# Assumed landing times of DMAs by kind of transfer in a scheduled forward-and-backward kernel

## The chip, the cores and the metric

The kernel runs on one core of a Trainium2 chip. Its time is the device time in microseconds of one execution; smaller is better. Before the change four executions took 803.83, 809.00, 809.76 and 813.18 us, median 809.38 us. One execution was profiled.

## The reference

A forward pass and the gradients of all its inputs. In the forward pass x has shape (2, 16000, 256), in bfloat16. Two convolutions over time of width 3, each followed by the tanh form of GELU and by keeping every second step, bring it to 4000 steps; then comes a joint of every step with eight vectors g:

```
h  = gelu(conv3(x, w1))[:, ::2]          # 2 x 8000 x 256
f  = gelu(conv3(h, w2))[:, ::2]          # 2 x 4000 x 256
fe = f @ w_f ;  ge = g @ w_g
j  = tanh(fe[:, :, None] + ge[:, None])  # 2 x 4000 x 8 x 256
out = j @ w_o
```

The outputs are out and, from grad_out of out's shape, the gradients of x, w1, w2, g, w_f, w_g and w_o. A gradient of a weight is a product over time: it wants time on the partitions of both operands. A product along the layer wants channels there. So most tensors are needed in both layouts, and the kernel turns them with DMA transposes.

## The kernel before, in words

**Tiling.** The 2 x 4000 steps are cut in 18 chunks. Chunk 0 has 256 steps, chunks 1 to 7 have 512, chunk 8 has the 160 that end batch 0; chunks 9 to 15 have 512, chunk 16 has 256 and chunk 17 has 160. Three stages work on different chunks at once. `stage_a` computes the convolutions and fe of the next chunk (XC is x in column layout, HT the first layer, FT the second, FE is fe). `stage_j` treats the joint of the current chunk in four pairs of the eight vectors: JT is j by columns, made on ScalarE (ACT), JR is j by rows, made by a sum on VectorE (DVE) and a tanh on ACT; GO_R is a piece of grad_out as loaded and GOT the same transposed. Products with WOT (from GOT) go into a sum over the eight vectors, ZS, and the last sum is NGFE, the negative gradient of fe. GWO collects the gradient of w_o in PSUM over the whole program. `stage_de` takes the chunk before through the layers backwards (GF, GH) and adds up the weight gradients ACCF, ACC2 and ACC1.

**Transposes.** All are issued from SyncE's (SP's) queue. FER is fe by rows, for JR. NFR, GFR and GHR are the gradients NGFE, GF and GH by rows; FR and HR are FT and HT by rows, kept from the forward pass until the gradients meet them. XC comes transposed from x in HBM, GOT from GO_R in SBUF. Plain loads (GO_R, X9 and X5, which are x by rows) and stores (OUT_SB, GX_SB, w_out) go through the same queue.

**Order.** Nothing is ordered by hand. Each operation is recorded with its engines, an assumed cost and its buffers; `Flow.issue` runs a model of the engines forwards (`run`) and backwards (`backward`) a few times and emits the program in the order of the best pass. In that model a compute operation may follow when its inputs are ready and a wake-up time has passed; an operation that would have to wait is treated as if it could start `SLACK` ns later than it could, so others are taken first. A DMA counts as landed when the queue's own share of its work is done, 2000 ns have passed and a margin has passed too:

```
o.done = ring[e] + 2000.0 + o.margin
```

The margin is `MARGIN` unless the call gives another (the first loads have `FIRST` or 2000 ns). It delays the readers in the planned order, and the moment at which a stored buffer is taken for free. It puts no wait in the program: on the chip everything waits on semaphores, in the order planned. An operation with two possible engines (copies out of PSUM, the squares JSQ) goes where the model has room.

Each class of buffers has a few slots: three for GOT, four for GO_R and w_out together, one for GHR. A transfer into a slot waits for the last reader of what was in it.

**The end.** In the last chunk `acc_add` writes each weight gradient as w_out on DVE and stores it; there are seven such stores. `store` writes two more.

Of the kernel before, what the change touches and what calls it, by code (L numbers as in the profile page):

```python
# [13 lines left out]
ACT = mybir.ActivationFunctionType  # L14
# [8 lines left out]
FIRST = 500.0  # L23
# [20 lines left out]
class Flow:  # L44
# [1 line left out]


    WAKE = {"PE": 45.0, "ACT": 25.0, "DVE": 25.0, "POOL": 280.0, "SP": 60.0}
    SLACK = {"PE": 800, "ACT": 300, "DVE": 300, "POOL": 0.0, "SP": 0.0}
    MARGIN = 4500.0  # L50
    TAIL = {"PE": 180.0, "ACT": 130.0, "DVE": 95.0, "POOL": 40.0, "SP": 0.0}

    def __init__(self, ctx, tc):
# [221 lines left out]
def c_dve(n, f=1.0):  # L275
    return 66.0 + 1.042 * n * f
# [3 lines left out]
def kernel(  # L280
# [27 lines left out]
    KT = 2  # L308
    P = 128
# [25 lines left out]
    F = Flow(ctx, tc)  # L335
# [99 lines left out]
    def dma(q, out, in_, r, w, bytes_, new=(), transpose=False, at=None, after=(), cost=None, hold=(), nb=None, margin=None):  # L435
        def go(e):
            eng_ = nc.sync if e == "SP" else nc.gpsimd if e == "POOL" else nc.scalar
            if transpose:
                return eng_.dma_start_transpose(out=out(), in_=in_())
            else:  # L440
                return eng_.dma_start(out=out(), in_=in_())
        c = 1260.0 if transpose else 400.0 if q == "SP" else cost or (750.0 if q == "POOL" else 100.0)
        return op(q, c, go, r=r, w=w, new=new, at=at, after=after, hold=hold, nb=nb, margin=margin,
                  work=bytes_ / 256 * 1.25 if transpose else bytes_ / 300.0)
# [6 lines left out]
    def load_xc(g_, at):  # L451
        b, ci, c0, W = chunks[g_]
        nb, wh, S = nb_of[g_], whole[g_], st[g_]
        XC = buf("jt", [P, 4 * KT * 2 * P], BF16, "XC0") if g_ == 0 else buf("xc", [P, 4 * KT * CW], BF16, "XC")
        if wh:
            vw = lambda: XC.t[:, 0:nb * 4 * KT * P].rearrange("p (a c k q) -> p a c k q", a=nb, c=4, k=KT)
            S["xcol"] = lambda c, kt: vw()[:, :, c, kt, :]
            S["xback"] = [(P, lambda kt: vw()[:, 0:nb - 1, 3, kt, :])]
            last_cols = lambda lo, hi: vw()[:, nb - 1, 3, :, lo - (nb - 1) * P:hi - (nb - 1) * P]
            src = x[b, 4 * c0:4 * (c0 + W), :].rearrange("(p r) d -> p (r d)", r=4 * nb)  # L460
            n = 2 * 4 * KT
            S["XCd"] = [dma("SP", lambda h=h: XC.t[:, h * n * P:(h + 1) * n * P].rearrange("p (g q) -> p g q", q=P),
                            lambda h=h: src[:, h * n * P:(h + 1) * n * P], r=[], w=[(XC, ("m", h))],
                            bytes_=n * P * P * 2, new=[XC] if h == 0 else [], transpose=True, at=at,
                            margin=FIRST if g_ < 2 else None) for h in range(nb // 2)]
            S["XCk"] = [(XC, ("m", h)) for h in range(nb // 2)]
        else:
            vw = lambda: XC.t[:].rearrange("p (g w) -> p g w", g=4 * KT)
            S["xcol"] = lambda c, kt: vw()[:, c * KT + kt, 0:W]
            S["xback"] = [(P, lambda kt: vw()[:, 3 * KT + kt, P - 1:W - 1])]  # L470
            last_cols = lambda lo, hi: vw()[:, 3 * KT:4 * KT, lo:hi]
            S["XCd"] = [dma("SP", lambda: vw()[:, :, 0:W], lambda: xr[b, c0:c0 + W, :], r=[], w=[(XC, ("m", 0))],
                            bytes_=W * 4 * D * 2, new=[XC], transpose=True, at=at)]
            S["XCk"] = [(XC, ("m", 0))]
        if ci > 0:
            xh = st[g_ - 1]["XH"]
            XS = shift("xs", g_, "XS", last_cols, [S["XCk"][-1]], lambda: xh[:], [xh], at=at)
        else:
            XS = shift("xs", g_, "XS", last_cols, [S["XCk"][-1]], None, [], at=at)
        S["xback"] = [(0, lambda kt: XS[:, kt, :])] + S["xback"]  # L480
        if c0 + W < MQ:
            XH = S["XH"] = buf("xh", [P, KT, 1], BF16, "x_halo")
            op("POOL", 200.0, lambda e: nc.gpsimd.tensor_copy(out=XH[:], in_=last_cols(W - 1, W)),
               r=[S["XCk"][-1]], w=[XH], new=[XH], at=at)
        S["XC"], S["XS"] = XC, XS
# [141 lines left out]
    def dma_rows(name, cls, g_, src, reads, n, nb=None, at=None):  # L627

        R = buf(cls, [P, KT * n * P if cls == "hrs" else KT * NB * P], BF16, name)
        R.view = lambda t_: t_[:, 0:KT * n * P].rearrange("p (k b q) -> p k b q", k=KT, q=P)  # L630
        R.rows = lambda m, bl: R[:m, :, bl, :]
        R.cols = lambda m, bl, d2: R[:m, d2, bl, :]
        dma("SP", lambda: R.t[:, 0:KT * n * P].rearrange("p (g q) -> p g q", q=P), src, r=reads, w=[R],
            bytes_=KT * n * P * P * 2, new=[R], transpose=True, nb=nb, at=at)
        return R

    def col_rows(name, cls, g_, SRC, keys, nb=None):
# [31 lines left out]
    def stage_a(g_, t0, dt):  # L669
# [4 lines left out]
        ns, nc_ = KT * (Wp + P), KT * Wp  # L674
# [13 lines left out]
        for nm, T_, k_, keys in (("HTo", HTo, (HT, "os"), [(HT, ("o", 0)), (HT, ("o", 1))]),  # L688
                                 ("G1o", G1o, (G1o, "s"), [(G1o, 0), (G1o, 1)])):
            if wh:  # L690
                op(("POOL", "DVE"), (430.0, c_dve(KT * (P - 1), 0.25)), lambda e, T_=T_: (
                    nc.gpsimd if e == "POOL" else nc.vector).tensor_copy(out=T_[:, :, 1:P], in_=T_[:, :, Wp:Wp + P - 1]),
                   r=keys, w=[k_])
# [4 lines left out]
            else:  # L698
                pv, pw, pk = st[g_ - 1][nm], P + chunks[g_ - 1][3], st[g_ - 1][nm + "k"]
                op("POOL", 200.0, lambda e, T_=T_, pv=pv, pw=pw: nc.gpsimd.tensor_copy(  # L700
                    out=T_[:, :, r0:r0 + 1], in_=pv[:, :, pw - 1:pw]), r=pk, w=[(k_[0], k_[1] + "h")])
# [21 lines left out]
        FE = colbuf("fe", g_, "FE")  # L723
        S["FE"] = FE
        n = nb_of[g_]
# [12 lines left out]
        if wh:  # L738
            FR_ = S["FER"] = buf("fer", [P, NB, D], BF16, "FER")
            dma("SP", lambda: FR_[:, 0:n].rearrange("p b (k q) -> p (b k) q", q=P), lambda: FE.t[:, 0:KT * n * P],  # L740
                r=[(FE, 0), (FE, 1)], w=[FR_], bytes_=KT * n * P * P * 2, new=[FR_], transpose=True)
        else:
            pad_tail(g_, FE)
            S["FER"] = to_rows("fer", FE, 0, n * P, [0, 1, "z"])
# [4 lines left out]
            bytes_=(ns + nc_) * P * 2, new=[HR], transpose=True, nb=late[0])  # L749
# [6 lines left out]
        else:  # L756
            R1 = buf("hrs", [P, KT * 2 * P], BF16, "HRs")
            assert nb_of[g_] == 2
            for kt in range(KT):
                dma("SP", lambda kt=kt: R1[:, kt * 2 * P:(kt + 1) * 2 * P].rearrange("p (g q) -> p g q", q=P),  # L760
                    lambda kt=kt: HTo[:, kt, P - 1:3 * P - 1],
                    r=[HT], w=[(R1, kt)], bytes_=2 * P * P * 2, new=[R1] if kt == 0 else [], transpose=True, nb=late[0])
            S["HRs"] = [R1], lambda m, bl, d2: R1[:m, d2 * 2 * P + bl * P:d2 * 2 * P + (bl + 1) * P]
        FR = col_rows("FR", "fr", g_, FT, ["z"], late[1])
# [147 lines left out]
    def acc_add(ACC, key, acc_ap, ps, g_, out):  # L912
        if g_ == NG - 1:
            t_ = buf("go", [P, NB, 2, V], BF16, "w_out")
            op("DVE", c_dve(512), lambda e: nc.vector.scalar_tensor_tensor(
                out=t_[:, 0].rearrange("p k d -> p (k d)"), in0=acc_ap().rearrange("p k d -> p (k d)"), scalar=-1.0, in1=ps[:],
                op0=ALU.mult, op1=ALU.subtract),
               r=[(ACC, key), ps], w=[t_], new=[t_])
            dma("SP", lambda: out.rearrange("(dt p) n -> p dt n", p=P),
                lambda: t_[:, 0], r=[t_], w=[], bytes_=131072)  # L920
        elif g_ == 0:
            evac(lambda: acc_ap().rearrange("p k d -> p (k d)"), lambda: ps[:], 512, r=[ps], w=[(ACC, key)])
        else:
            op("DVE", c_dve(512), lambda e: nc.vector.tensor_tensor(  # L924
                out=acc_ap().rearrange("p k d -> p (k d)"), in0=acc_ap().rearrange("p k d -> p (k d)"), in1=ps[:],
                op=ALU.add), r=[(ACC, key), ps], w=[(ACC, key)])

    def stage_de(g_, t0, dt):
# [9 lines left out]
        nc_ = KT * nb_of[g_] * P  # L938
# [9 lines left out]
        for mt in range(KT):  # L948
            ps = psum()

            def mms(e, mt=mt, ps=ps):
# [4 lines left out]
                out=GF[:, mt, 0:W], in0=S["G2"][:, mt, :W], scalar=1.0, in1=ps[:, :W], op0=ALU.add, op1=ALU.mult),  # L956
               r=[(S["G2"], mt), ps], w=[(GF, mt)])
# [5 lines left out]
        if not last:  # L963
            FH = S["GFh"] = buf("gfh", [P, KT, 1], BF16, "GF_halo")
            op("POOL", 200.0, lambda e: nc.gpsimd.tensor_copy(out=FH[:], in_=GF[:, :, W - 1:W]),
               r=[(GF, 0), (GF, 1)], w=[FH], new=[FH])
# [4 lines left out]
        for mt in range(KT):  # L971
            ps = psum()

            def mms(e, mt=mt, ps=ps):
# [9 lines left out]
                out=GHo[:, mt, 0:Ws], in0=S["G1o"][:, mt, r0:r0 + Ws], scalar=1.0, in1=ps[:, 0:Ws], op0=ALU.add, op1=ALU.mult),  # L984
               r=S["G1b"](mt) + [ps], w=[(GH, ("o", mt))])
# [3 lines left out]
            def mms2(e, mt=mt, ps=ps):  # L989
# [4 lines left out]
                out=GHe[:, mt, 0:W], in0=S["G1e"][:, mt, 0:W], scalar=1.0, in1=ps[:, :W], op0=ALU.add, op1=ALU.mult),  # L994
               r=[(S["G1e"], mt), ps], w=[(GH, ("e", mt))])
# [7 lines left out]
        if not last:  # L1003
            hh = S["GHh"] = buf("ghh", [P, KT, 1], BF16, "GHe_halo")
            op("POOL", 200.0, lambda e: nc.gpsimd.tensor_copy(out=hh[:], in_=GHe[:, :, W - 1:W]),
               r=[(GH, ("e", 0)), (GH, ("e", 1))], w=[hh], new=[hh])
# [28 lines left out]
        else:  # L1035
# [2 lines left out]
        ghk = [(GH, (k_, mt)) for k_ in "oe" for mt in range(KT)] + [(GH, "ez"), (GH, "oz")]  # L1038
        GHR = buf("ghr", [P, 2 * KT * CW], BF16, "GHR")
        dma("SP", lambda: GHR.t[:, 0:2 * nc_].rearrange("p (g q) -> p g q", q=P), lambda: GH.t[:, 0:2 * nc_], r=ghk, w=[GHR],  # L1040
            bytes_=2 * nc_ * P * 2, new=[GHR], transpose=True)
        for o_, nm in ((0, "GHoR"), (nc_, "GHeR")):
            R_ = S[nm] = part(GHR, lambda t_, o_=o_: t_[:, o_:o_ + nc_].rearrange("p (k b q) -> p k b q", k=KT, q=P))
            R_.rows = lambda m, bl, R_=R_: R_[:m, :, bl, :]
# [10 lines left out]
        for bl, m in sblk:  # L1055
# [28 lines left out]
            elif wh:  # L1084
                if head == 1:
                    dma(STOREQ, lambda: out_1[b, 1:5, :].rearrange("(o f) d -> o f d", o=1), lambda GX=GX: GX[0:1],
                        r=[gk(0), gk(1)], w=[], bytes_=2048, cost=550.0)
                for lo, hi in row_parts(head, P):
# [3 lines left out]
                        bytes_=(hi - lo) * 4096, cost=550.0)  # L1092
            else:
                for lo, hi in row_parts(r0, r1):
# [3 lines left out]
                        bytes_=(hi - lo) * 2048, cost=550.0)  # L1098
# [15 lines left out]
    def gg_out():  # L1114
# [43 lines left out]
       r=[(warm, 0)], w=[(warm, 1)])  # L1158
# [117 lines left out]
```

## Time and profile before

The profiled execution took 806.12 us; its span is 804.3 us.

| Engine | busy us | share of the span |
|---|---|---|
| TensorE, matmul (PE) | 772.1 | 96% |
| TensorE, weight loads (PEld) | 568.0 | 71% |
| VectorE (DVE) | 746.4 | 93% |
| ScalarE (ACT) | 696.7 | 87% |
| GpSimd (POOL) | 84.5 | 11% |

A chain of waits and works, followed back from the last instruction, puts 32% of the span on TensorE and 7% on DVE in what it shows. The queue of DMAs moved 187.81 MB. From issue to landing the median was 6.2 us for GOT, 5.2 for NFR, 5.9 for XC, 3.8 for FER, 4.1 for GFR and FR, 4.6 for GHR and 4.8 for HR.

In the lines of the profile a number with L is a line of the kernel (L413 is the matmul helper, L439 and L441 issue a transpose and a plain DMA). "ps<-NFR,FR" names what is written and read. "x8" counts instructions. In lists of waits the columns are the total, the number and the longest wait in microseconds. In a timeline the first column is the start and the second the duration; "[2.19 <-DMA NFR<-NGFE]" is idle time ahead of an instruction and what ended it. SPq is SP's queue of DMA issues; its bars are the issuing, and the landing comes later.

### The profile page before, as it was taken

To read this page: it belongs to the slowest core of one execution; us is meant where nothing else is said; L and a number is where in the kernel's file an instruction comes from. 1 tells how busy PE (TensorE), PEld (TensorE's weight loads), DVE (VectorE), ACT (ScalarE), POOL (GpSimd) and SP (SyncE) were. 2 spreads that over 40 slices of the span, in tenths; PEclk is the share of its full clock that TensorE was granted. 3 is DMA by queue.
4 is the path that set the end of the run, shared out by engine and by line. 5 is a ranking of instruction groups with operands and counts; after the bars stand their busy time and mean duration, and the time that the engine had idled before them with its cause. 6 is when DMAs were issued, how large, how long until landed. Compare 5 with 4: busy or idle time off the path is not lost. (4 is left out here: it accounts for less than half of the span.)

```text
span 804.3 us, 16636 instructions
## 1 busy us (share of the span) xinstructions
PE 772.1 (96%) x6004; PEld 568.0 (71%) x6004; DVE 746.4 (93%) x1702; ACT 696.7 (87%) x1150; POOL 84.5 (11%) x269
## 2 busy tenths in 40 slices
PE   7798999999898999999999989999999999999996
PEld 5455767686675867777776658676776867778885
DVE  3999999999988999998979999998999999999975
ACT  4999999998887998988778999988889989998762
POOL 2101010100101001011101110000001001001111
PEclk9999999999999999999999999999999999999999
DMA  8999999999999999999999999999999999999986
GB/s 193 201 257 207 240 200 238 245 214 265 231 222 231 240 268 220 268 225 227 254 230 199 238 231 235 256 236 239 261 237 253 236 285 233 252 245 241 215 208 164
DMA packets 419231, 187.81 MB, mean 234 GB/s; under 512 B 342182, under 2 KB 410828, under 8 KB 419148
## 3 DMA queue, kind: packets, MB, share of 16 engines
q1 hardware_dynamic: 416636, 185.54, 104.4%
q10 hardware_dynamic: 2384, 1.18, 0.6%
q8 instruction: 47, 0.77, 0.4%
q14 instruction: 36, 0.29, 0.1%
q0 software_dynamic: 128, 0.03, 0.0%
HBM read 51.56 MB, written 50.34 MB: 127 GB/s over the span
## 5 line engine op out<-in xcount | busy, mean ns | idle before, releaser
L800 ACT ACTIVATE JT<-FE,GE 128x512 bf16<-128x512 bf16 (+2 forms) x288 | 186.0, 699 | 1.0 <-DVE FE L429 0.9
L820 ACT ACTIVATE JR<-JR 128x1024 bf16<-128x1024 bf16 x128 | 137.3, 1081 | 20.3 <-DVE JR L813 20.1
L867 DVE SCALAR_TENSOR_TENSOR NGZ<-JSQ,ps 128x512 f32<-128x512 bf16 (+2 forms) x252 | 151.3, 606 | 2.8 <-PE ps L413 2.7
L413 PE MATMUL ps<-WO,JT 128*128 128x256 bf16 x1024 | 150.3, 273 | 3.2 <-ACT JT L800 2.1
L413 PE MATMUL ps<-GOT,WT 128*128 128x512 bf16 (+3 forms) x640 | 151.4, 333 | 1.8 <-DVE OUT_SB L429 1.2
L424 ACT CAST OUT_SB<-ps 128x512 bf16<-128x512 f32 x210 | 126.5, 615 | 24.0 <-PE ps L413 23.7
L413 PE MATMUL GWO<-GO_R,JR 128*128 128x256 bf16 x1024 | 135.4, 277 | 5.9 <-ACT JR L820 5.9
L875 DVE TENSOR_TENSOR ZS<-ZS,NGZ 128x512 f32<-128x512 f32 (+2 forms) x216 | 130.7, 611 | 0.7
L413 PEld LDWEIGHTS <-JT 128*128 128x128 bf16 x1024 | 98.4, 98 | 46.0 <-ACT JT L800 4.2
L413 PEld LDWEIGHTS <-JR 128*128 128x128 bf16 x1028 | 101.2, 99 | 31.2 <-ACT JR L820 7.7
L413 PEld LDWEIGHTS <-WT 128*128 128x128 bf16 x1000 | 88.4, 98 | 43.4 <-issue 5.6
L857 ACT ACTIVATE JSQ<-JT 128x1024 bf16<-128x1024 bf16 (+2 forms) x113 | 109.6, 972 | 7.0 <-DVE NGZ L867 6.4
L413 PEld LDWEIGHTS <-W 128*128 128x128 bf16 x720 | 66.8, 99 | 54.8 <-issue 4.4
L413 PE MATMUL ps<-WT,GH 128*128 128x256 bf16 x732 | 98.9, 273 | 0.1
L413 PE MATMUL ps<-XC,W 128*128 128x512 bf16 (+4 forms) x432 | 93.6, 346 | 2.6 <-DMA XC<-in_x_dram 2.6
L813 DVE TENSOR_TENSOR JR<-FER,GEB 128x1024 bf16<-128x1024 bf16 x128 | 87.1, 686 | 9.6 <-DMA FER<-FE 8.6
L413 PE MATMUL ps<-GHR,X 128*128 128x256 bf16 x768 | 91.5, 273 | 2.1 <-DVE NGZ L867 1.3
L413 PEld LDWEIGHTS <-X 128*128 128x128 bf16 x768 | 74.8, 98 | 13.1 <-issue 2.2
L605 DVE SCALAR_TENSOR_TENSOR g_s<-g_sq,ps 128x512 bf16<-128x512 bf16 (+2 forms) x108 | 65.7, 610 | 18.8 <-ACT HT L603 14.7
L413 PEld LDWEIGHTS <-GH 128*128 128x128 bf16 x732 | 71.2, 98 | 14.9 <-DVE GH L983 0.6
L601 ACT ACTIVATE g_sq<-ps 128x512 bf16<-128x512 f32 (+2 forms) x108 | 60.3, 558 | 19.9 <-PE ps L413 13.4
L924 DVE TENSOR_TENSOR ACC<-ACC,ps 128x512 f32<-128x512 f32 x96 | 64.2, 678 | 9.7 <-PE ps L413 9.2
(124 smaller groups left out, 964.4 us busy)
## 6 DMA issues: line engine op xcount, KB each, us to landing
GO_R<-in_grad_out_dram SPq DMA_DIRECT2D x56, 512.0 KB, 4.6
out_dram<-OUT_SB SPq DMA_DIRECT2D x56, 512.0 KB, 5.2
out_dram<-GX_SB SPq DMA_DIRECT2D x28, 512.0 KB, 3.5
X<-in_x_dram SPq DMA_DIRECT2D x14, 576.0 KB, 6.2
X<-in_x_dram SPq DMA_DIRECT2D x14, 512.0 KB, 6.8
GO_R<-in_grad_out_dram SPq DMA_DIRECT2D x8, 256.0 KB, 4.0
out_dram<-OUT_SB SPq DMA_DIRECT2D x8, 256.0 KB, 3.9
GOT<-GO_R SPq DMA_TRANSPOSE x72, 6.2
```

What stands on the lines that cost most here:

```text
L413: nc.tensor.matmul(ps_ap, lhsT=lhsT, rhs=rhs, start=start, stop=stop)
L424: nc.scalar.copy(out=dst(), in_=src())
L601: op("ACT", c_act(W, True), lambda e, mt=mt, ps=ps: nc.scalar.activation(out=sq[:, mt, :W], in_=ps[:, :W], func=ACT.Square, scale=GELU_SQR ...
L605: op("DVE", c_dve(W), lambda e, mt=mt, ps=ps: nc.vector.scalar_tensor_tensor(out=s[:, mt, :W], in0=sq[:, mt, :W], scalar=1.0, in1=ps[:, :W ...
L800: op("ACT", c_act(W, ptr=True), lambda e, j=j, mt=mt: nc.scalar.activation(out=S["blocks"](JT[:, j, mt, :W]), in_=S["fe"](mt), func=ACT.Ta ...
L813: op("DVE", c_dve(n * 2 * D, 0.5), lambda e, lo=lo, n=n, m=m, JR=JR: nc.vector.tensor_tensor(out=JR[:m, lo % 2:lo % 2 + n], in0=S["FER"][: ...
L820: op("ACT", c_act(n * 2 * D), lambda e, lo=lo, n=n, m=m, JR=JR: nc.scalar.activation(out=JR[:m, lo % 2:lo % 2 + n], in_=JR[:m, lo % 2:lo % ...
L857: nc.scalar.activation(out=JSQ[:, :, :W], in_=JT[:, j, :, :W], func=ACT.Square)
L867: op("DVE", c_dve(W) + 6, lambda e, d2=d2, ps=ps, u=u, zap=zap, JSQ=JSQ: nc.vector.scalar_tensor_tensor(out=zap(), in0=JSQ[:, d2, :W], sca ...
L875: op("DVE", c_dve(W), lambda e, d2=d2, dst=dst, NGZ=NGZ: nc.vector.tensor_tensor(out=dst[:, d2, :W], in0=ZS[:, d2, :W], in1=NGZ[:, :W], op ...
L924: op("DVE", c_dve(512), lambda e: nc.vector.tensor_tensor(out=acc_ap().rearrange("p k d -> p (k d)"), in0=acc_ap().rearrange("p k d -> p ( ...
```

## The change

Three constants and five calls are touched.

- `MARGIN` goes from 4500 to 3500 ns and TensorE's `SLACK` from 800 to 500 ns.
- A margin `LATE` of 8000 ns is new. It is given to XC from the third chunk on (in whole chunks), FER, NFR, GFR and GHR, and to what else `dma_rows` transposes, other than FR.
- The shorter `MARGIN` remains for GOT after the first chunk, GO_R, the row loads of x, FR, HR and all stores.
- The seven stores of `acc_add` are issued from ACT's queue instead of SP's, with an assumed cost of 450 ns.

```diff
-    SLACK = {"PE": 800, "ACT": 300, "DVE": 300, "POOL": 0.0, "SP": 0.0}
-    MARGIN = 4500.0
+    SLACK = {"PE": 500, "ACT": 300, "DVE": 300, "POOL": 0.0, "SP": 0.0}
+    MARGIN = 3500.0
+    LATE = 8000.0
...
-                            margin=FIRST if g_ < 2 else None) for h in range(nb // 2)]
+                            margin=FIRST if g_ < 2 else F.LATE) for h in range(nb // 2)]
...
-            bytes_=KT * n * P * P * 2, new=[R], transpose=True, nb=nb, at=at)
+            bytes_=KT * n * P * P * 2, new=[R], transpose=True, nb=nb, at=at, margin=None if name == "FR" else F.LATE)
...
-                r=[(FE, 0), (FE, 1)], w=[FR_], bytes_=KT * n * P * P * 2, new=[FR_], transpose=True)
+                r=[(FE, 0), (FE, 1)], w=[FR_], bytes_=KT * n * P * P * 2, new=[FR_], transpose=True, margin=F.LATE)
...
-            dma("SP", lambda: out.rearrange("(dt p) n -> p dt n", p=P),
-                lambda: t_[:, 0], r=[t_], w=[], bytes_=131072)
+            dma("ACT", lambda: out.rearrange("(dt p) n -> p dt n", p=P),
+                lambda: t_[:, 0], r=[t_], w=[], bytes_=131072, cost=450.0)
...
-            bytes_=2 * nc_ * P * 2, new=[GHR], transpose=True)
+            bytes_=2 * nc_ * P * 2, new=[GHR], transpose=True, margin=F.LATE)
```

Because the planner is run anew with these numbers, the order changes throughout the program on every engine, and some copies and squares go to another engine. The instructions' number and sizes stay the same, apart from where they run.

## The prediction

> **What bounds the kernel now.** I read the page's engine shares first, then the busy times stage by stage, then TensorE's waits, and last the timeline around the longest of them.
>
> ```profile
> PE 772.1 (96%) x6004; PEld 568.0 (71%) x6004; DVE 746.4 (93%) x1702; ACT 696.7 (87%) x1150; POOL 84.5 (11%) x269
> ...
> core 0: us, PE busy (x) PEld busy (x) DVE busy (x) ACT busy (x) POOL busy (x), PEclk, DMA share, GB/s
> 20.00:88.00 68.00, 57.48 (x390) 38.28 (x388) 64.83 (x162) 65.14 (x110) 7.52 (x20) 0.95 1.04 217
> 88.00:203.00 115.00, 115.00 (x849) 81.67 (x848) 112.51 (x236) 109.23 (x173) 11.02 (x30) 1.00 1.09 239
> 203.00:265.00 62.00, 57.31 (x413) 40.31 (x411) 56.02 (x117) 49.49 (x78) 6.94 (x20) 0.97 1.12 226
> 265.00:370.00 105.00, 105.00 (x849) 80.57 (x848) 103.57 (x230) 95.74 (x159) 10.06 (x34) 1.00 1.11 242
> 370.00:480.00 110.00, 104.97 (x823) 74.28 (x822) 99.35 (x239) 95.01 (x156) 13.16 (x42) 1.00 1.03 230
> 480.00:780.00 300.00, 299.38 (x2395) 227.24 (x2393) 287.57 (x659) 265.55 (x447) 28.13 (x96) 1.00 1.07 243
> ```
>
> TensorE never stops from 88 to 203, 265 to 370 and 480 to 780 us. Eight GWO matmuls of 256 columns follow each other in 0.87 us there (the chain), 0.109 us each; at that rate the whole program is 755 us of matmul. What can be won is idle time: 10.5 us from 20 to 88 (DVE and ACT full: a ramp), 4.7 from 203 to 265, 5.0 from 370 to 480, 0.6 after, 7.0 in the last 24.3. The middle ones have a name:
>
> ```profile
> PE ps L413 <- DMA NFR<-NGFE: 7.1, 3, 2.5
> PE GWO L413 <- ACT JR L820: 0.9, 2, 0.5
> PE ps L413 <- DVE g_sq L613: 0.7, 1, 0.7
> ...
> 187.71 0.69 DVE L875 TENSOR_TENSOR NGFE<-ZS,NGZ 128x512 bf16<-128x512 f32 x1
> ...
> 192.72 5.45 SPq L439 DMA_TRANSPOSE GOT<-GO_R  x1
> ...
> 198.27 0.56 SPq L441 DMA_DIRECT2D GO_R<-in_grad_out_dram  x1
> ...
> 198.89 0.62 SPq L441 DMA_DIRECT2D out_dram<-OUT_SB  x1
> ...
> 199.60 2.38 SPq L439 DMA_TRANSPOSE NFR<-NGFE  x1
> ...
> 206.96 1.05 PE L413 MATMUL ps<-NFR,FR 128*128 128x256 bf16 x8 [2.19 <-DMA NFR<-NGFE]
> ```
>
> NGFE is whole at 188.4 us; its transpose gets its turn on SP at 199.60, 11.2 us later, because SP issues DMAs back to back and is that far behind; it lands 7.3 us after. The plan allowed 2.0 + 4.5 us and the transfer's own work. It was 2.2 us short.
>
> **What the Trainium skill says.** "Perfetto Trace Analysis", DMA Instruction — HWDGE: the record of a DMA issue starts when its semaphores are satisfied and covers descriptor generation, not data movement. The trace agrees: the GOT issue at 185.44 lasts 6.10 us though its buffer was free at 175.9, so SP's bars are work and not waits. "TensorE: Matmul & The Clock Gate", What's actually happening: an idle window of about 3.4 us puts the array at half clock. Here the stall that ended at 256.4 us is followed by 256.5 to 260.3 us at a granted 0.55; those at 207 and 476 us, as long, by none. "DMA: Bandwidth & Descriptors", Issuing engines are not separate DMA queues: a second ring saves the sequencer's time only. No run of before shows it for these stores.
>
> **The change part by part.** The sum is made against the profiled execution: 806.1 us, span 804.3; the median of the runs is 809.4, 3.3 higher.
>
> *Late-needed transposes, 4.5 to 8.0 us (NFR, GFR, GHR, FER, XC).* The planner places the consumer 3.5 us later. In the order that the two builds give TensorE I added up the matmuls (0.109 us per 256 columns) between the last WOT product of a chunk, which NGFE needs, and the first matmul that reads NFR. It goes from 19.5 to 24.1 us in chunks 3 and 4, 16.2 to 19.5 in 7, 16.8 to 19.2 in 8, 16.1 to 20.0 in 9. These are the chunks that stalled; their stalls were 2.3, 2.7, 0.9, 0.3 and 2.6 us from start to start, so each is covered with 1.3 to 2.4 us to spare. The group of NFR matmuls shows 8.0 us of idle time in all, GHR in the middle 0.4; the half clock after 256.5 costs 3.8 x 0.45 = 1.7. Gone: 10.1 us. XC's margin costs nothing: by the landings its first reader comes 10 us or more after it past the ramp.
> What is late next: with TensorE 8 us faster SP has less time to catch up, and these stalls were its catching up. If SP's lag grows by the first stall removed (2.2 us), chunk 4 is at its limit. Bounds 0 to 5 us; I take 1.5, because from 480 to 780 us SP kept up with a TensorE that stood still for 0.6 us.
> FER: after the batch change DVE waited 2.5 us for it and ACT then 4.5 for JR; the work from FE to the first GWO product on JR goes from 15.6 to 21.1 us there, so the 0.9 us of GWO waits go: -0.9.
>
> *Loads ahead, 4.5 to 3.5 us (GOT, GO_R, X9, HR, FR, and the slots that stores free).* The dangerous one is GOT. Its longest way from a free buffer to landing is 9.5 us on SP and 9.0 more (free 175.9, issued 185.44, landed 194.4): 18.5. Matching landings with matmuls, GOT had 0.8 us left at its tightest in the steady part (issued 637.8), 2.5 and 2.7 at 593 and 624. The matmul work between the release and the first reader shrinks from 21.8 to 19.4 us at two of these places, which would leave -1.6 and 0.1. Against it, there the new order issues GOT ahead of HR, whose issue is some 3 us (3.05 at 633.39). Bounds 0 to 6 us (three short waits and a half clock); I take 1.5. GO_R lands 16.8 us or more before its matmul through the middle, HR and FR 23 or more: a shorter margin costs nothing while that stays.
>
> *TensorE's slack, 800 to 500 ns.* Products may follow their ACT or DVE producers 0.3 us closer. Such waits are now 0.9 + 0.7 + 0.6 us from 88 to 780. Bounds: 0 to 4 us; a gain isn't likely, as TensorE is full there anyway. I take 1.4.
>
> *Work between engines.* The planner moves 8 squares JSQ from DVE (31 to 23, 0.60 us each) to ACT (113 to 121, 0.95 each). DVE's queue is 6 us shorter, ACT's 7.6 longer. ACT is hidden (265.6 of 300 us busy at 480 to 780); its cost appears only where ACT is full, up to 140 us. Up to the end of chunk 1's gradient (NGFE at 97.3 us) DVE has 1.5 us less queued, ACT the same, TensorE 0.7 less: the ramp takes -1.0 (bounds -3 to +2; its PE stalls of 3.4 and 1.0 us may move).
>
> *The last gradients on ACT's ring.* Seven stores leave SP:
>
> ```profile
> 796.41 5.40 SPq L441 DMA_DIRECT2D out_dram<-w_out  x7
> ...
> DVE w_out L915 <- DMA out_dram<-w_out: 2.0, 2, 1.1
> ```
>
> SP had the GX_SB stores (794.97, 1.35 us) ahead of them. On ACT they stand behind four GX_SB copies, and nothing stands behind them. The first goes out up to 1.1 us sooner (its DVE result was there at 795.3), so the buffers that DVE waits for come free sooner; but the last product ends near 799.8 us and the last DVE step began at 800.7, so at most 0.7 can go. An ACT issue costs about what SP's does (0.38 to 0.66 us in the first 12 us, 0.4 on SP). The order before it changes as well: after the last WOT product TensorE has 12.6 us of matmul left instead of 11.3, but the X-gradients of the chunk before now stand between GH and GX, ahead of the last GHR transpose that needs their buffer. Followed step by step, these two cancel to 0.3 us. Together -0.6 (bounds -2 to +1.5).
>
> Sum: -10.1 + 1.5 - 0.9 + 1.5 + 1.4 - 1.0 - 0.6 = -8.2 us: 797.9 us for an execution like the profiled one. The runs of before spread over 9 us; if late landings make the spread, the added room draws the median towards the lower end, so I take the 3.3 us for gained too: **798 us**.
>
> **Rivals.** (1) *Forecast*, 798, 792 to 803: chance 0.55. (2) *SP is the real bound.* It is as full as TensorE, its lag is 6 to 11 us from 100 to 720, and no DMA work is removed; each stall taken from NFR comes back at the next transpose. A third of the gain stays: 809.4 - 3.4 = 806. For it: the lag of 11 us before every NFR stall. Against: 300 us at full rate with that lag steady. Chance 0.22. (3) *GOT becomes the stall, slower.* Every whole chunk has a GOT with about 19.4 us of cover; it decides when release to landing is over that, and 18.5 is already seen. At 1.6 us in each of 14 whole chunks that is +22 us, less the 10.1 won: 809 + 12 = 821. Against: only a few of the 72 had under 3 us. Chance 0.13. (4) *Nothing to see.* Both orders are full, the list is only shuffled and gains and new small waits cancel: 809. Chance 0.10.
>
> **How the numbers follow.** About 1% (8 us) is what a measurement of this kernel tells from no change. Faster by over 1% is under 801.3: most of case 1, 0.45, and the fast edges of the others, 0.05. Slower by over 1%: case 3 and a tail of 4, 0.15. The rest, 0.35, is within. The range reaches from case 1's lower end with no new wait at all (791) over case 2 and most of 4 (811); case 3 is left out.
>
> **What would show it.** NFR waits of TensorE under 2 us in sum; no half clock past 100 us; 203 to 265 us with under 1 us idle; SP's lag before NFR as before or longer; GOT waits of TensorE under 2 us; JSQ on DVE 23. I am wrong if TensorE waits for GOT in most chunks, if its waits for ACT and DVE grow past 4 us, or if the ramp up to 88 us loses over 3 us more.

## The result, and the profile after

The changed kernel takes 801.55 us (median of 44 executions, 797.37 to 807.66) against 808.44 us for the kernel before beside it (63 executions, 800.46 to 815.71). The ratio is 0.9934, 95% interval 0.9919 to 0.995: 0.7% less, 5.3 us by the ratio and 6.9 by the medians, where 8 to 11 were forecast. Here and below a median is over all executions of a kernel, while a ratio compares only those in the faster of the two states that executions of this kernel show, so it isn't the quotient of two medians. The profiled execution took 803.75 us, its span is 801.9 (before: 806.12 and 804.3).

Engine shares of the page, then busy times stage by stage, TensorE's waits from 88 to 780 us, and the timeline around the longest stall, all of the changed kernel:

```profile
PE 771.5 (96%) x6004; PEld 567.3 (71%) x6004; DVE 743.6 (93%) x1691; ACT 703.8 (88%) x1158; POOL 91.4 (11%) x272
```

```profile
20.00:88.00 68.00, 58.50 (x404) 39.23 (x402) 65.83 (x165) 66.16 (x111) 7.33 (x18) 0.95 1.04 220
88.00:203.00 115.00, 114.39 (x838) 80.64 (x837) 113.31 (x236) 109.21 (x171) 12.26 (x32) 1.00 1.08 237
203.00:265.00 62.00, 62.00 (x468) 45.18 (x467) 61.08 (x128) 54.92 (x86) 7.10 (x20) 1.00 1.08 241
265.00:370.00 105.00, 103.59 (x830) 78.58 (x828) 100.34 (x222) 91.97 (x155) 10.68 (x33) 1.00 1.09 238
370.00:480.00 110.00, 105.84 (x824) 75.00 (x823) 99.19 (x236) 98.47 (x163) 15.05 (x46) 0.98 1.03 233
480.00:780.00 300.00, 295.40 (x2364) 223.52 (x2362) 282.58 (x649) 266.79 (x443) 31.00 (x95) 1.00 1.09 242
```

```profile
PE ps L414 <- DMA GOT<-GO_R: 7.9, 4, 3.4
PE GWO L414 <- ACT JR L821: 1.4, 6, 0.3
PE ps L414 <- DVE NGZ L868: 0.6, 1, 0.6
PE ps L414 <- DVE OUT_SB L430: 0.4, 1, 0.4
PE ps L414 <- DVE NGFE L876: 0.2, 1, 0.2
```

```profile
391.44 5.98 SPq L440 DMA_TRANSPOSE XC<-in_x_dram  x2
397.52 0.53 SPq L442 DMA_DIRECT2D out_dram<-OUT_SB  x1
398.14 2.78 SPq L440 DMA_TRANSPOSE GHR<-GH  x1
401.01 1.93 SPq L440 DMA_TRANSPOSE GOT<-GO_R  x1
...
402.62 0.32 PE L414 MATMUL ps<-GOT,WT 128*128 128x128 bf16 x4
406.35 1.03 PE L414 MATMUL ps<-GOT,WT 128*128 128x512 bf16 x2 [3.41 <-DMA GOT<-GO_R]
```

The stall of 203 to 265 us is gone (62.00 of 62 us busy), and no wait for NFR is left in the list, where 7.1 us stood. In its place TensorE waits for GOT, four times, 7.9 us in all: 3.4 us up to 406.35 (after XC and GHR on SP, and 5.3 us to landing), 3.3 up to 598.6, and two short ones up to 359 and 646.5 (0.4 and 0.8). Behind the longest the granted clock is 0.61 from 406 to 410 us, which costs 1.6 us more; behind the one at 598.6 it is 1.00. So the waits for DMAs from 88 to 780 us are 7.9 us after as against 7.5 before (8.2 with one of 0.7 that the list puts down to DVE's g_sq, though what came last for that matmul was NFR).

In this pair of profiles TensorE's idle time from 88 to 780 us didn't fall at all: it is 10.3 us before and 10.8 after. The 2.4 us by which the span is shorter come from the ramp up to 88 us, where idle time fell by 1.0, from the end after 780 (1.2 less) and from busy time (0.6 less). In a second pair, e8 and e5 below, whose spans differ by 3.6, idle time from 88 to 780 fell from 17.7 to 14.0 us; both of these traces lack 44 of the matmul records, which makes their idle time too large. The removed stalls are certain; that they are what made the time shorter has to come from the experiments.

### The profile page after: what moved, and what is told of

It is laid out like the page before. It is cut to its first block, busy times and chain, and to the rows that moved or that the text cites. A ratio compares the mean times of both kernels' runs of the same rounds, so it can differ in the third digit from the quotient of the medians.

```text
span 801.9 us, 16648 instructions
## 1 busy us (share of the span) xinstructions
PE 771.5 (96%) x6004; PEld 567.3 (71%) x6004; DVE 743.6 (93%) x1691; ACT 703.8 (88%) x1158; POOL 91.4 (11%) x272
## 2 busy tenths in 40 slices
DMA packets 419231, 187.81 MB, mean 234 GB/s; under 512 B 342182, under 2 KB 410828, under 8 KB 419148
## 4 chain that ended last, share of the span: by engine, by line
PE 70%; DVE 14%; ACT 8%; DMA 4%; issue 2%; SPq 0%; POOL 0%; ACTq 0%; POOLq 0%; DVEq 0%
PE ps L414 60%; PE GWO L414 10%; DVE NGZ L868 3%; DMA GOT<-GO_R 2%; DVE ZS L876 2%; ACT JR L821 2%; DVE g_s L606 1%; DMA W<-in_w_dram 1%; DVE JR L814 1%; ACT JT L801 1%; ACT g_sq L602 1%; ACT JSQ L858 1%; DVE g_sq L617 1%; DVE OUT_SB L430 1%; ACT GX_SB L427 1%
## 5 line engine op out<-in xcount | busy, mean ns | idle before, releaser
L801 ACT ACTIVATE JT<-FE,GE 128x512 bf16<-128x512 bf16 (+2 forms) x288 | 182.0, 689 | 0.8 <-DVE FE L430 0.7
L821 ACT ACTIVATE JR<-JR 128x1024 bf16<-128x1024 bf16 x128 | 135.4, 1073 | 24.1 <-DVE JR L814 23.7
L425 ACT CAST OUT_SB<-ps 128x512 bf16<-128x512 f32 x206 | 120.8, 608 | 28.0 <-PE ps L414 27.5
L414 PE MATMUL GWO<-GO_R,JR 128*128 128x256 bf16 x1024 | 133.6, 274 | 4.6 <-ACT JR L821 4.5
L414 PEld LDWEIGHTS <-WT 128*128 128x128 bf16 x1000 | 88.5, 98 | 57.5 <-DMA GOT<-GO_R 10.1
L858 ACT ACTIVATE JSQ<-JT 128x1024 bf16<-128x1024 bf16 (+2 forms) x121 | 116.8, 965 | 9.5 <-DVE NGZ L868 8.3
L414 PE MATMUL ps<-XC,W 128*128 128x512 bf16 (+4 forms) x432 | 91.8, 342 | 1.4 <-DMA XC<-in_x_dram 1.4
L414 PEld LDWEIGHTS <-GH 128*128 128x128 bf16 x732 | 71.1, 98 | 14.8 <-issue 0.6
L925 DVE TENSOR_TENSOR ACC<-ACC,ps 128x512 f32<-128x512 f32 x96 | 64.2, 678 | 12.9 <-PE ps L414 12.6
L427 ACT ACTIVATE GX_SB<-ps 128x512 bf16<-128x512 f32 x105 | 62.0, 615 | 7.3 <-PE ps L414 6.9
```

What stands on the lines that cost most here:

```text
L414: nc.tensor.matmul(ps_ap, lhsT=lhsT, rhs=rhs, start=start, stop=stop)
L425: nc.scalar.copy(out=dst(), in_=src())
L427: nc.scalar.activation(out=dst(), in_=src(), func=ACT.Copy, scale=scale)
L801: op("ACT", c_act(W, ptr=True), lambda e, j=j, mt=mt: nc.scalar.activation(out=S["blocks"](JT[:, j, mt, :W]), in_=S["fe"](mt), func=ACT.Ta ...
L821: op("ACT", c_act(n * 2 * D), lambda e, lo=lo, n=n, m=m, JR=JR: nc.scalar.activation(out=JR[:m, lo % 2:lo % 2 + n], in_=JR[:m, lo % 2:lo % ...
L858: nc.scalar.activation(out=JSQ[:, :, :W], in_=JT[:, j, :, :W], func=ACT.Square)
```

## The experiments

Three theories stand behind the expectations, and cover is the number that they argue about. *A*: what decides is the cover that the order gives a transfer, counted in matmul work between what releases it and its first reader (for GOT from the last reader of its buffer on; it also needs its input GO_R, which can land later); the long margin gives it to NFR, and thin cover of GOT gives a part back. Cover can be set against what a transfer needs: its lag on SP, which is the time from that release to the issue, and the way from issue to landing. *B*: SP's lag is the bound, and a stall only moves. *C*: the slack or the new order as such (operations that happen to follow each other better) gives the gain. Each margin or slack that is altered makes the planner order the program anew; only e4, e7 and e10 keep an order, and e8 keeps it up to the end. The kernel before took 813.53 us on the chip of e1 to e4, 809.39 on that of e5 to e8 and 810.07 on that of e9 to e12.

**One part alone.** e1, the long margin alone, in this call and the other three that the change gives it to:

```diff
+    LATE = 8000.0
...
-            bytes_=KT * n * P * P * 2, new=[R], transpose=True, nb=nb, at=at)
+            bytes_=KT * n * P * P * 2, new=[R], transpose=True, nb=nb, at=at, margin=None if name == "FR" else F.LATE)
```

> Only the 8000 ns margin for NFR, GFR, GHR, FER and XC; GOT and the plain loads keep 4500 ns, TensorE's slack 800 ns, the last gradients SP's queue. The order is planned anew; counted in it, the matmul work between NGFE's last product and NFR's first reader is 20 us or more but for one place of 15.1, and the work between GOT's buffer coming free and its first reader is 14.5 and 14.9 us at two places, 17.8 or more at the others. Theory A (the long margin works, and GOT's cover is what gives the gain back): NFR waits of TensorE 0 to 2.5 us in sum, GOT waits 3 to 7 us at the two thin places, time 800 to 804, ratio about 0.993. Theory B (SP's lag is the bound, a stall only moves): some 7 to 9 us of DMA waits in all, spread over GOT, NFR and others, 805 to 808. Theory C (slack and the new order give the gain): no gain here, 807 to 809.

Measured 807.9 us, ratio 0.9938 (0.991 to 0.9965). TensorE's waits from 88 to 780 us:

```profile
PE ps L414 <- DMA GOT<-GO_R: 6.7, 3, 3.8
PE psb L659 <- POOL FE L647: 1.8, 1, 1.8
...
PE ps L414 <- DMA NFR<-NGFE: 0.8, 1, 0.8
```

The sizes are those that A gave (3 to 7 us for GOT, under 2.5 for NFR), and so is the ratio. Its time of 800 to 804 us is missed, on a chip where the kernel before takes 813.5. Of the two places that A had named as thin only one stalls. The GOT issued at 402 us has 14.9 us of cover and needs 18.9 (lag 14.6, landing 4.3); it is 4.0 short, and the wait, the longest, is 3.8. The one issued at 439 us has 14.5 and needs 12.6 (6.1 and 6.5): no wait. So cover alone decides nothing; it decides against lag and landing.

The two other GOT waits, of 1.4 us each up to 357.5 and 644.3 us, came at places that hadn't looked thin, with 22.2 and 25.5 us of work since the buffer's last reader. There it was the input that came late: GO_R landed 9.1 and 12.8 us after the buffer was free. From that landing GOT needed 14.7 and 15.4 us, and TensorE came for it after 13.3 and 14.0. A transfer is released by the later of its buffer and its input, and cover counts from there.

B's sum of DMA waits holds (8.5 us from 88 to 780), and its time (805 to 808 of 809, a ratio of 0.995 or more) isn't shut out by the interval. GOT's waits are there with its margin still at 4500 ns, so the number as such isn't their cause.

e2, the short margin alone (`LATE` stands in the same four calls and keeps the old 4500 ns there):

```diff
-    MARGIN = 4500.0
+    MARGIN = 3500.0
+    LATE = 4500.0
```

> Only the margin 3500 ns for everything that has no margin of its own but NFR, GFR, GHR, FER and XC, which keep 4500 ns; slack 800 ns, last gradients on SP. Counted in the order: NFR's cover is 14.8, 14.9, 16.8 us at its thinnest (as before the change), GOT's 18.3 or more. Theory A: TensorE waits 5 to 8 us for NFR as before and under 2 us for GOT, because cover in the order and not the margin's number decides; 806 to 810, ratio 1.00. If the short margin by itself costs GOT waits: 4 us or more of them, 810 to 815. Theory B: 7 to 9 us of DMA waits, whichever the place, 808.

807.82 us, ratio 0.9947 (0.9923 to 0.997). The time lies in A's range; its ratio of 1.00 is missed, and so are B's 7 to 9 us of DMA waits:

```profile
PE ps L414 <- DMA NFR<-NGFE: 3.3, 2, 2.4
PE ps L414 <- DVE NGZ L868: 1.7, 3, 1.0
PE ps L414 <- DVE g_s L621: 1.0, 1, 1.0
PE GWO L414 <- ACT JR L821: 0.8, 2, 0.6
PE ps L414 <- DMA GOT<-GO_R: 0.8, 1, 0.8
```

The list gives NFR 3.3 us from 88 to 780, but two of the waits that it puts down to DVE belong to NFR as well:

```profile
252.33 1.03 PE L414 MATMUL ps<-NFR,FR 128*128 128x256 bf16 x8 [1.00 <-DVE g_s L621]
...
711.49 1.03 PE L414 MATMUL ps<-NFR,FR 128*128 128x256 bf16 x8 [0.96 <-DVE NGZ L868]
```

At both, what these matmuls need of DVE had been done 2 us or more before, and they start 0.14 us after NFR landed. So NFR costs 5.2 us, the lower end of A's 5 to 8, and GOT 0.8 (1.4 with one that is put down to ACT): the short margin brings no more GOT waits by itself. The expectation had looked at the thinnest cover only, which is as before. Where SP's lag is long, in chunks 3 to 5 (10 to 12 us from the whole NGFE), NFR's cover from the last product went from 19.6 us to 20.9, 19.6 and 20.9 in the new order. Chunk 4, which kept its 19.6, stalls for 1.0 us; the other two don't stall. That fits A with the lag counted in.

What e2 leaves open is its gain. Its DMA waits are 6.6 us in all, against 8.2 in the profile of the kernel before, which is too little for a ratio of 0.9947. The two parts alone (0.9938 and 0.9947) are each worth nearly the whole change (0.9934), within wide intervals; they don't add up. That the new order gives something in another way, as C has it, isn't shut out here.

e8, the last gradients on ACT's ring:

```diff
-            dma("SP", lambda: out.rearrange("(dt p) n -> p dt n", p=P),
-                lambda: t_[:, 0], r=[t_], w=[], bytes_=131072)
+            dma("ACT", lambda: out.rearrange("(dt p) n -> p dt n", p=P),
+                lambda: t_[:, 0], r=[t_], w=[], bytes_=131072, cost=450.0)
```

> The kernel before, with the seven last gradient stores issued from ACT's queue and nothing else; up to them the order is that of before. Theory A, by the prediction's step: at most 0.7 us less, ratio 0.999 to 1.001, NFR waits of 5 to 9 us as before. If the ring alone gives part of the gain: the time from the last matmul to the end falls by over 1.5 us, ratio under 0.998.

810.52 us, 1.0009 (0.9983 to 1.0036). The ring's part is nothing that can be measured.

e9, the slack alone:

```diff
-    SLACK = {"PE": 800, "ACT": 300, "DVE": 300, "POOL": 0.0, "SP": 0.0}
+    SLACK = {"PE": 500, "ACT": 300, "DVE": 300, "POOL": 0.0, "SP": 0.0}
```

> The kernel before with TensorE's slack 500 ns instead of 800 and nothing else; the order is planned anew. Counted in it: NFR's cover 13.5, 14.4, 15.0 us at its thinnest (14.9, 14.9, 16.1 before), GOT's 15.3, then 18.3 (17.0). Theory A (cover decides): NFR waits of 8 us or more, some GOT wait, TensorE's waits for ACT and DVE up by up to 1.4 us: 808 to 813, ratio 1.000 to 1.005. Theory C (the slack gives part of the gain): ratio under 0.997.

812.33 us, 1.0032 (1.0014 to 1.0051): slower by 2.6 us by the ratio. C has no gain here: not every new order gains. The waits from 88 to 780 us, the first seven:

```profile
PE ps L413 <- DVE NGFE L875: 3.6, 6, 1.2
PE ps L413 <- DMA NFR<-NGFE: 2.5, 2, 2.3
PE ps L413 <- DVE NGZ L867: 2.0, 2, 1.3
PE ps L413 <- DMA GOT<-GO_R: 1.7, 1, 1.7
PE ps L413 <- DMA GFR<-GF: 1.6, 3, 0.9
PE ps L413 <- ACT FT L603: 1.6, 1, 1.6
PE ps L413 <- ACT OUT_SB L424: 1.6, 3, 0.8
```

TensorE follows ACT and DVE more closely and waits for them: 13.5 us in all by the list, where it was 2.2 before. Some 3.2 us of these stand ahead of readers of NFR, GFR and GHR that had only just landed; put down to the transfers, the waits for ACT and DVE are 10.3 us, those for DMAs 9.1, and NFR's 4.1. The first is far over what A allowed (1.4 more than before), and NFR is far under A's 8. DVE also has 15 instructions more than before (x1717 on the page): this order shares out the work otherwise, too.

**Cover for GOT.** e3:

```diff
-            new=[GOT], transpose=True, at=at, margin=2000.0 if g_ == 0 else None)
+            new=[GOT], transpose=True, at=at, margin=2000.0 if g_ == 0 else 6500.0)
```

> The changed kernel with one number more: GOT after the first chunk has a margin of 6500 ns instead of 3500. Counted in its order: GOT's cover 18.7 us or more instead of 14.2, NFR's 18.2 or more as in the changed kernel; squares on DVE fall further. Theory A: GOT waits under 1 us, NFR waits under 1 us, no half clock past 100 us, 6 to 10 us less than the changed kernel: 792 to 796, ratio to before about 0.982. Theory B: the waits that leave GOT come back at NFR, FER, GHR or XC, 6 us or more of DMA waits from 88 to 780, 800 to 803. Theory C: 801 as the changed kernel, whatever the waits do.

805.61 us, 0.9911 (0.9883 to 0.9938). GOT's waits from 88 to 780 us fall from 7.9 to 1.9 us, NFR's are 1.6, and the granted clock is 1.00 throughout that stretch: A's direction, though not its size (792 to 796 us, 0.982), and the interval overlaps that of the changed kernel. DMA waits of 3.5 us, not 6, speak against B. But the span of the profiled execution is only 1.0 us under that of the changed kernel. The trace says where the rest went: the last sum of chunk 16's NGFE starts at 763.5 us against 768.3 in the changed kernel, 4.8 us earlier, and that of chunk 17 at 782.1 against 783.8. So 3.1 us are lost in the last chunk, whose order had changed too, and 0.7 after it. e6 keeps the old margin there:

```diff
-            new=[GOT], transpose=True, at=at, margin=2000.0 if g_ == 0 else None)
+            new=[GOT], transpose=True, at=at, margin=2000.0 if g_ == 0 else 6500.0 if g_ < 15 else None)
```

> As e3_got65, but the 6500 ns for GOT hold only for chunks 1 to 14; in its order the end is that of the changed kernel (12.5 us of matmul work after the last GOT reader; 11.2 in e3_got65), the middle that of e3_got65. Theory A: the last chunk's NGFE comes 4 to 5 us earlier than in the changed kernel as in e3_got65 for chunk 16, and the tail doesn't give it back: span 796 to 798, ratio to before 0.986 to 0.989. Theory B: no less than e5_after_again, within 2 us. If it was the ramp's half clock and not the tail that cost e3_got65 its gain: 800 to 801 with a clock under 0.95 up to 88 us.

> The changed kernel once more, beside the next three on one chip. All theories: 0.993 of before, GOT waits of TensorE of 5 to 10 us at about 403, 595 and 645 us, since its order is the same; if the GOT waits fall elsewhere by 10 us or more, they belong to the execution and not to the order.

> e6_got65_to_14 once more, beside the last three on another chip: 0.9915 of before if e6 was typical, DMA waits of TensorE under 4 us from 88 to 780. If e6's low waits were chance, they are 6 us or more.

e5, the changed kernel on the same chip: 803.48 us, 0.9931 (0.9906 to 0.9957). e6: 799.9 us, 0.9915 (0.9881 to 0.9949), a span of 798.8, with chunks 16 and 17 at 763.8 and 779.3 us. A's 0.986 to 0.989 and its span of 796 to 798 are missed narrowly. e12, the same kernel on another chip: 799.16 us, 0.987 (0.9834 to 0.9906). Waits of e12 from 88 to 780 us:

```profile
PE ps L414 <- DMA GOT<-GO_R: 2.2, 3, 1.6
PE ps L414 <- DVE NGFE L876: 1.4, 1, 1.4
PE ps L414 <- DMA NFR<-NGFE: 0.8, 1, 0.8
PE GWO L414 <- DMA GO_R<-in_grad_out_dram: 0.8, 1, 0.8
```

The DMA waits are 2.7 us (e6) and 3.8 (e12) where the changed kernel has 7.9 and, in e5, 8.2. Both medians lie under 800 us. On e5's chip e6 is 3.6 us under e5 by the medians but 1.3 by the ratios, and the intervals overlap, so by e6 alone the gain over the changed kernel isn't shown, nor B's "within 2 us" shut out; e12's interval lies below that of the changed kernel's first measurement. In e5 the GOT stalls came at 401 and 592 us again, but were 1.8 and 2.8 us instead of 3.6 and 3.5 from start to start, and one of 2.7 us at 775 us was new: the order makes the thin places, the execution decides how much each costs. The place at 401 has 14.2 us of cover in this order. It needed 17.6 us in the first profile (lag 12.3, landing 5.3) and was 3.4 short, as long as the wait; in e5 it needed 15.9 (11.5 and 4.4) and was 1.7 short, and the wait was 1.7.

e11, more for all:

```diff
-    LATE = 8000.0
+    LATE = 9000.0
...
-            new=[GOT], transpose=True, at=at, margin=2000.0 if g_ == 0 else None)
+            new=[GOT], transpose=True, at=at, margin=2000.0 if g_ == 0 else 6500.0 if g_ < 99 else None)
```

> The changed kernel with 6500 ns for GOT after the first chunk and 9000 ns instead of 8000 for the long margin. Counted in its order: NFR's cover 18.3, then 19.4 and 21.4 us, GOT's 18.0 at one place and more elsewhere in the middle, the end as in the changed kernel. Theory A: DMA waits of TensorE under 3 us from 88 to 780, 797 to 800, ratio 0.984 to 0.989, at least e12's. If cover for all is bought with SP's time or with waits for ACT and DVE: 0.992 or more with over 5 us of those waits.

805.16 us, 0.9938 (0.9899 to 0.9977). DMA waits are 3.2 us, just over A's 3, but A's time and ratio are missed: the waits for ACT, DVE and GpSimd are 9.3 us (2.6 in the changed kernel), as the other branch has it. In this order cover for all is bought with waits for the other engines.

**What makes SP late.** e4 takes bytes away, in the changed kernel's order; e10 does so in that of the kernel before. In both, 64 stores of OUT_SB write 8 of their 128 partitions, so most of the output out is left unwritten: they are probes and no kernels to use. e7 keeps the bytes and moves the issuing of these 64 stores to GpSimd (two of the three pieces of its edit are shown):

```diff
-                dma(STOREQ, lambda: rows_, lambda: OUT[:, 0:nb_of[g_]].rearrange("p a u v -> p a (u v)"), r=[OUT], w=[],
+                dma(STOREQ, lambda: rows_[0:8], lambda: OUT[0:8, 0:nb_of[g_]].rearrange("p a u v -> p a (u v)"), r=[OUT], w=[],
```

```diff
-            eng_ = nc.sync if e == "SP" else nc.gpsimd if e == "POOL" else nc.scalar
+            eng_ = nc.gpsimd if other else nc.sync if e == "SP" else nc.gpsimd if e == "POOL" else nc.scalar
...
-                    bytes_=W * 1024)
+                    bytes_=W * 1024, other=True)
```

> The changed kernel in its own order, with one difference: a store of OUT_SB of a whole chunk writes 8 of its 128 partitions, so most of the output out is left unwritten and about a fifth of the bytes and their descriptors leave SP's queue. Orders on TensorE, DVE, ACT and GpSimd are the same. Theory A: SP's lag falls by several us, and with it the GOT waits (7.9 us to under 1): 6 to 10 us less than the changed kernel, 792 to 796; the ramp to 88 us, where ACT and DVE are full, stays. Theory B: SP sets the pace everywhere, so the ramp and the tail gain too: under 788. Theory C: 800 or more.

> The kernel before in its own order, with one difference: a store of OUT_SB of a whole chunk writes 8 of its 128 partitions, as in e4_less_stores, so most of the output out is left unwritten. If the whole gain of the change is that late landings are better covered, the two orders are worth the same once nothing lands late: no DMA waits from 88 to 780 us, ratio to before within 0.003 of e4_less_stores's 0.976. If the changed order is better in itself (ramp, FER, squares moved from DVE, tail: 2.5 us in the prediction): ratio 0.979 or more. If SP's lag is not what makes the NFR waits: over 3 us of them stay.

> The changed kernel in its own order, the same bytes; the stores of OUT_SB of whole chunks are issued from GpSimd's queue instead of SP's (60 instructions leave SP). It asks whether SP's lag is the issuing or the transfers. If it is the issuing: SP's lag before NFR falls by 4 us or more, GOT waits under 2 us, 793 to 797. If it is the transfers themselves, which stay: lag before NFR 10 to 14 us as in the changed kernel, GOT waits 6 us or more, 800 to 804. GpSimd's copies of halo columns then stand behind stores; if TensorE comes to wait for them, 805 or more.

e4: 793.17 us, 0.9757 (0.9709 to 0.9805). e10: 790.75 us, 0.976 (0.9724 to 0.9797). 158.32 MB instead of 187.81 were moved, 16% less and not a fifth. e10's busy times by stage:

```profile
88.00:203.00 115.00, 115.00 (x845) 81.42 (x843) 113.68 (x238) 109.76 (x173) 12.86 (x34) 1.00 0.98 205
203.00:265.00 62.00, 62.00 (x472) 45.67 (x471) 60.87 (x127) 55.32 (x87) 6.74 (x18) 1.00 1.00 213
265.00:370.00 105.00, 105.00 (x850) 80.34 (x849) 101.51 (x226) 93.12 (x157) 10.55 (x36) 1.00 0.88 198
370.00:480.00 110.00, 108.79 (x858) 78.36 (x856) 105.14 (x250) 101.85 (x166) 12.42 (x41) 1.00 1.02 209
480.00:780.00 300.00, 299.12 (x2411) 227.81 (x2409) 286.27 (x668) 258.63 (x437) 35.47 (x101) 0.99 0.90 196
```

And the stretch of its timeline in which NFR stood 11 us in the kernel before:

```profile
183.57 5.20 SPq L439 DMA_TRANSPOSE GOT<-GO_R  x1
...
184.67 0.69 DVE L875 TENSOR_TENSOR NGFE<-ZS,NGZ 128x512 bf16<-128x512 f32 x1
...
188.87 0.58 SPq L441 DMA_DIRECT2D GO_R<-in_grad_out_dram  x1
189.51 0.77 SPq L441 DMA_DIRECT2D out_dram<-OUT_SB  x1
190.37 1.28 SPq L439 DMA_TRANSPOSE NFR<-NGFE  x1
```

NFR has its turn 5.0 us after NGFE is whole, where it was 11.2, and in neither kernel does TensorE wait for any DMA from 88 to 780 us. The two orders are then worth the same: the ratios differ by less than 0.001, with intervals that allow some 5 us either way. That is what A expects, that the margins give no gain where nothing is late, and it speaks against C. It isn't proof, as the gain in question is itself 5 to 7 us, so a better order worth nearly that much is only just outside. Fewer bytes also change more than the late landings: of the 15.6 us by which e10's span is shorter than that of the kernel before, 8.2 are idle time from 88 to 780 us, about what its DMA waits were there; 1.1 are idle time up to 88, 3.2 idle time after 780 and 3.1 busy time. B's "under 788" for e4 isn't reached (its profiled span is 792.2).

e7: 804.95 us, 0.9976 (0.9948 to 1.0003), against e5's 803.48 and 0.9931 on the same chip: no faster, and slower is likely but not shown, since the intervals overlap. With the stores issued from GpSimd, and the bytes as they were, SP's lag before NFR, counted from the whole NGFE, is 12.9, 16.7 and 16.4 us in chunks 2 to 4 (12.4, 13.8 and 14.6 in the changed kernel), and one wait for NFR is longer than any in the other kernels shown here:

```profile
242.91 8.42 SPq L440 DMA_TRANSPOSE GOT<-GO_R  x1
251.42 0.57 SPq L442 DMA_DIRECT2D GO_R<-in_grad_out_dram  x1
252.08 4.25 SPq L440 DMA_TRANSPOSE NFR<-NGFE  x1
...
264.58 1.87 PE L414 MATMUL ps<-NFR,FR 128*128 128x256 bf16 x8 [6.46 <-DMA NFR<-NGFE]
```

SP isn't late for having to issue these stores: with them gone, the issues that stay take longer (8.42 us for one GOT), and e4 and e10, with fewer bytes, are early. So the transfers make it late. This is what the Trainium skill, "DMA: Bandwidth & Descriptors", section Issuing engines are not separate DMA queues, says of a second queue: it shares the same engines.

## Why the prediction was right, and where not

The time was forecast at 798 us and is 801.55; faster, as the likeliest case had it, and with the first half of its mechanism, NFR's stalls gone. The second half failed: the new cover was to cost 1.5 us at GOT, and cost 9.5. With what was measured for each term the sum is -10.1 for NFR, nothing for the lag before NFR, 9.5 for GOT, 0.4 for the slack, 0.5 for FER, some -1.2 for the ramp and nothing for the end: about -1 us where the prediction has -8.2. The profiled spans agree with that more nearly (-2.4) than with the time (-5 to -7). So the terms don't account for most of the gain in time, and that it came out so near the forecast is in part luck.

- **NFR and GHR, -10.1: right.** Stalls and half clock of 203 to 265 us are gone in both profiles of the changed kernel.
- **SP's lag, +1.5: right in kind, at the wrong place.** Before NFR, from the whole NGFE to the issue, it went from 11.2, 12.6 and 12.4 us in chunks 3 to 5 to 13.8, 14.6 and 14.8, and NFR still landed 1.5 us or more before its reader there. The longer lag was paid for at GOT and not at NFR. (In the kernel before this lag was 5.7 to 13.1 us in chunks 2 to 14, where rival 2 says 6 to 11.)
- **GOT, +1.5: the step that failed.** It measures 7.9 us of waits and 1.6 of half clock, where 0 to 6 was the range; the sign that was to show the forecast right, GOT waits under 2 us, didn't come. Two of the places had been named, issues at 637.8 and 593 us with -1.6 and 0.1 us left. They came, at 646 and 595 us, but with the sizes the other way round: 0.9 and 3.5 us from start to start.

  What shrank there isn't the work since the buffer's last reader, as the step has it (25.7 us at both places before, 26.2 and 24.9 after). It is the time from the landing of GO_R, which GOT transposes, until TensorE comes for GOT: from 19.5 to 12.6 us and from 17.8 to 13.7. GOT then needed 13.3 and 17.0 us. In all four waits of the changed kernel GO_R landed after the buffer was free, by 1.8 to 13.6 us. GO_R's loads stand in the same queue, and their own lag grew from 10.5 to 17.0 us and from 10.4 to 14.3. The step put GO_R's shorter margin at nothing, because it lands 16.8 us or more before its matmul; but GOT's transpose reads it first. At the longer of the two stalls:

```profile
575.16 0.60 SPq L442 DMA_DIRECT2D GO_R<-in_grad_out_dram  x1
...
589.92 4.22 SPq L440 DMA_TRANSPOSE HR<-HT  x1
594.19 1.84 SPq L440 DMA_TRANSPOSE GOT<-GO_R  x1
...
598.59 0.61 PE L414 MATMUL ps<-GOT,WT 128*128 128x512 bf16 x2 [3.31 <-DMA GOT<-GO_R]
```

  By the trace's semaphores this GO_R landed at 581.6 us, 11.1 after the buffer was free. For the same reason the step's longest way to landing, 18.5 us, is counted from a release too early: the buffer of the GOT issued at 185.44 was free at 174.8 (not 175.9), but GO_R landed only at 181.6, which leaves 12.8. And HR, which the step expected behind GOT in the new order, stands ahead of it at both places.

  The largest stall, at 403 us, wasn't among the named places, because the step looked at the steady part alone: at the change of batch the new order leaves GOT 14.2 us of cover, and XC and GHR stand ahead of it on SP. With its half clock that is 5.2 of the 9.5 us.
- **Slack, +1.4:** e9, the slack alone, costs 2.6 us, within the bounds of 0 to 4. In the changed kernel the waits for ACT and DVE from 88 to 780 us are 2.6 us against 2.2.
- **Ramp, -1.0: right.** Chunk 1's last NGFE sum starts at 96.1 us (95.5 in e5) against 97.3.
- **FER, -0.9: not gained.** GWO's waits for JR are 1.4 us where they were 0.9. DVE's own waits for FER fell from 8.6 to 3.0 us over the whole program.
- **Ring and end, -0.6: not gained.** From the last NGFE to the end it is 18.1 us before, and 18.1 and 20.0 in the two profiles after; e8 shows nothing either.
- **The 3.3 us between profile and median: in part.** The fastest execution lies 8.0 us under the median before and 4.2 under it after, and the spread fell from 15.3 to 10.3 us; so the median did move towards the lower end, and by more than the profiled executions did. That late landings make the spread is likely, as e10's four executions lie within 1.6 us (789.44 to 791.05) where before has 803.0 to 818.04 beside it, but the missing bytes could do it in another way; and it isn't shown that the 10.3 us that are left come from GOT.

Rival 2 was nearer than its time of 806 says: taken as a sum, TensorE's waits for DMAs from 88 to 780 us went from 7.5 to 7.9 us in the first pair of profiles (from 8.2 if each wait is put down to what came last) and from 10.1 in e8 to 8.2 in e5. e6 and e12 show that this is no law: with cover for GOT too they are 2.7 and 3.8. Rival 3 came at its places, but at four and not in every chunk. What stays open is where the rest of the gain lies: the two spans differ by 2.4 us (3.6 for e8 and e5), the medians by 5.9 to 6.9, and one profile of each can't tell.

## What to carry to other kernels

Where one queue issues all transfers and is 10 us behind, set the cover of each transfer (the work between its release and its first reader) against its lag and landing, at every place and not at the thinnest alone. Count the release from the later of buffer and input: an input that is itself loaded through the queue comes later when the queue is later. After lengthening the cover of one kind, look at the kind with the next thinnest, which now meets a longer lag. Cutting the bytes without touching the order gives a rough upper bound of what better cover could be worth: here 2.4%, since ramp, end and busy time gained as well, of which the change took 0.7 and GOT's margin up to 0.6 more. In this case a second queue was no cure, because the transfers themselves were what was late.

## What the runs showed of the hardware

- The issue of one NFR transpose took 1.28 us with 16% fewer bytes in all, and 2.38 us in the kernel before at the same place. The bar of a DMA issue isn't a fixed cost here: it was longer in the run with more bytes under way, though its input had been whole for 11 us when it began.
- A stall of 3.4 us at 406 us was followed by a granted clock of 0.61 for 4 us, one of 3.3 us at 598.6 by none; in the kernel before one of 2.5 us at 256.6 was followed by 0.55 for 3.8 us, those of 2.2 and 2.4 us at 207 and 476 by none. Neither the half clock nor the length of stall that brings it was fixed here.
- With 64 stores moved from SP's queue to GpSimd's and the bytes unchanged, SP's lag before NFR didn't fall (12.9, 16.7 and 16.4 us in chunks 2 to 4, against 12.4, 13.8 and 14.6), and the median way of GOT from issue to landing grew from 5.3 to 8.1 us.
